# Channel attention and a relu² feed-forward: the later batches' folded weights by seven block products

## The chip, the cores and the metric

The kernel runs on one core of a Trainium2 chip. The metric is the device time of one execution in microseconds (us). A run's time here is that of the whole execution; the profiled execution also has a span, from its first to its last recorded instruction.

## The reference, cut to what matters

There are B = 4 batches of N = 6080 tokens with C = 256 channels, and F = 2048 hidden features, all float32.

```python
qn = q / (norm(q, axis=1) + 1e-6)          # norms over the tokens
kn = k / (norm(k, axis=1) + 1e-6)
s = kn.transpose(0, 2, 1) @ qn / tau       # 256 x 256 for each batch
a = softmax(s)                             # over the last axis
x = v @ a                                  # (4, 6080, 256)
h = maximum(x @ w_in, 0)                   # 256 -> 2048
out = (h * h) @ w_out                      # 2048 -> 256
```

## The kernel before

**Folding.** Since x only meets w_in, the kernel forms W = a w_in once a batch (256 x 2048) and computes v W. W is made in four groups g of 512 features. `eT` is the transposed softmax before its division by the row sums; the factor `rinv` (one over the row sum) is applied where W leaves PSUM.

**Precision.** TensorE takes float32 in a rounded form (fp32r). Every operand is therefore kept as a high part and a low part (`w_hi`, `w_lo`; `wi_hi`, `wi_lo`; `eT_hi`, `eT_lo`; `g_hi`, `g_lo`), and every product is three: high by high, high by low, low by high. The high part is a copy by ScalarE that rounds, the low part a difference by VectorE. For W the pair is the eviction of a PSUM tile: ScalarE writes `w_hi` (PSUM times `rinv`), VectorE then `w_lo` (PSUM times `rinv` less `w_hi`).

**The main loop.** A batch's tokens are cut into 12 blocks n (ten of 512 tokens, two of 480), and a block has 16 steps f, one for each 128 features, two steps a pair r. In a step `first_product` puts v W into a PSUM tile `ps_h` (6 matmuls of 512 columns) and ScalarE evicts it with relu into `x`. After a pair, `squares_and_sums` lets ScalarE square x, VectorE form sums of its blocks (`x<-x`), and both make `g_hi` and `g_lo`. The second product, two pairs later (LAG = 2), multiplies them with w_out by seven block products instead of eight (Strassen's scheme, `seven_products`; the sums of w_out are `wS`), into two PSUM tiles `ps_o`. At a block's end ScalarE copies `ps_o` out (`o<-ps_o`), and VectorE combines the pieces (`o<-o`).

**What runs beside it.** Batch b+1's attention and its W are generators, `attention(b)` and `softmax_and_W(b)`. The main loop takes one piece of them, up to the next `yield`, in each step but two of each block; in even steps right after `first_product`, in odd steps at the step's end. A group of the next batch's W may only be written once the last block of this batch is through with the old one (`may_write_W`), so its four groups are made during the last block, 11, and the start of the next batch's block 0. The softmax of batch 1 falls in blocks 8 and 9 of batch 0.

**PSUM.** There are eight banks: four for two `ps_o` tiles, three for `ps_h` (its three buffers also take the tiles of W and of the softmax), and one for the gram matrix, `ps_g`.

**Order.** Every engine carries out its instructions in the order in which the program issues them: `InProgramOrder` pins it, and so every row of the trace names its line, L27. The engines wait for each other by semaphores. The stretches of W in the old form are these lines of `softmax_and_W`:

```python
for h in range(NC):
    products(h)
    if h == NC - 1 and g + 1 < NG:
        wi[g + 1] = reload_w_in(b, g + 1)
    yield
    evict(h)
    yield
```

`products(h)` is six matmuls of 512 columns into one `ps_h` buffer (named `ps_w`), `reload_w_in` fetches the two parts of w_in's next group from a copy in DRAM.

Of the kernel before, what the change touches and what calls it, by code (L numbers as in the profile page):

```python
# [8 lines left out]
F32 = mybir.dt.float32  # L9
F32R = mybir.dt.float32r  # L10
# [20 lines left out]
def kernel(  # L31
# [25 lines left out]
    P = 128  # L57
# [92 lines left out]
    scratch = ctx.enter_context(tc.tile_pool(name="scratch", bufs=1, space=bass.MemoryType.DRAM))  # L150
    wi_kept = [[scratch.tile([P, NC, GRP], F32, name=f"wi_kept{g}_{i}") for i in range(2)] for g in range(NG)]

    def wi_tiles(b, g):
        hi = pool.tile([P, NC, GRP], F32R, tag="wi_hi", name=f"wi_hi{b}_{g}", bufs=1)
        lo = pool.tile([P, NC, GRP], F32R, tag="wi_lo", name=f"wi_lo{b}_{g}", bufs=1)
        return hi, lo
# [73 lines left out]
    def reload_w_in(b, g):  # L230
        parts = wi_tiles(b, g)
        for kept, part in zip(wi_kept[g], parts):
            nc.sync.dma_start(part.bitcast(F32), kept)
        return parts

# [139 lines left out]
    def attention(b):  # L375

        if b not in grams:
            grams[b] = Gram(b)
        g = grams[b]
        c0 = HEAD if b == 1 else 0  # L380
        for c in range(c0, min(c0 + QK_BUFS, g.n)):
            g.load(c)
        yield
        for c in range(c0, g.n):
            yield from until_even()
            p, jn, _ = g.q[c]
            hi = pool.tile([P, 2, J, C], F32R, tag="qk_hi", name=f"qk_hi{b}_{c}", bufs=1)
            lo = pool.tile([P, 2, J, C], F32R, tag="qk_lo", name=f"qk_lo{b}_{c}", bufs=1)
            h_, l_, r_ = (x[:p, :, :jn, :] for x in (hi, lo, g.raws[c]))
            scalar.copy(h_, r_)  # L390
            vector.tensor_sub(l_, r_, h_.bitcast(F32))
            yield
            yield from until_even()
            g.squares(c)
            g.add_squares(c)
            if c + QK_BUFS < g.n:
                g.load(c + QK_BUFS)
            for _ in g.products(c, [(hi, hi), (hi, lo), (lo, hi)]):
                yield
        yield from softmax_and_W(b)  # L400

    def pause(b, first, other):

        for _ in range(other if b else first):
            yield

    def softmax_and_W(b):
        gram, acc = grams[b].gram, grams[b].acc
        wi = {0: reload_w_in(b, 0)} if b else {}

        vector.tensor_add(acc[:, :, 0, :], acc[:, :, 0, :], acc[:, :, 1, :])
        yield from pause(b, 1, 2)
# [72 lines left out]
        vector.tensor_copy(eT_hi, ps_tv)  # L485
        vector.tensor_sub(eT_lo, ps_tv, eT_hi.bitcast(F32))
        yield from pause(b, 2, 3)

        for g in range(NG):
            while (b, g) not in may_write_W:  # L490
                yield
            if b == 0:
                while g not in wi_first:
                    yield
                hi, lo = wi_first.pop(g)
                keep_w_in(g, (hi, lo))
            else:
                hi, lo = wi.pop(g)
            w_hi = wpool.tile([P, NC, GRP], F32R, tag="w_hi", name=f"w_hi{b}_{g}")
            w_lo = wpool.tile([P, NC, GRP], F32R, tag="w_lo", name=f"w_lo{b}_{g}")  # L500
            ps_w = {}

            def products(h, terms=range(3)):
                if h not in ps_w:
                    ps_w[h] = ps_h.tile([P, T], F32, tag="h", name=f"ps_w{b}_{g}_{h}")
                for i in terms:
                    et, wt = ((eT_hi, hi), (eT_lo, hi), (eT_hi, lo))[i]
                    for d in range(NC):
                        tensor.matmul(
                            ps_w[h][:, 0:GRP],  # L510
                            et[:, d, h * P : (h + 1) * P],
                            wt[:, d, :],
                            start=i == 0 and d == 0,
                            stop=i == 2 and d == NC - 1,
                        )

            def evict(h):
                ps = ps_w.pop(h)[:, 0:GRP]
                scalar.activation(w_hi[:, h, :], ps, AF.Copy, scale=rinv[:, h : h + 1])
                vector.scalar_tensor_tensor(  # L520
                    w_lo[:, h, :],
                    ps,
                    rinv[:, h : h + 1],
                    w_hi[:, h, :].bitcast(F32),
                    op0=ALU.mult,
                    op1=ALU.subtract,
                )

            if b == 0:
                for h, terms in ((0, (0, 1)), (1, (0,)), (0, (2,)), (1, (1, 2))):  # L530
                    products(h, terms)
                yield
                for h in range(NC):
                    evict(h)
            else:
                for h in range(NC):
                    products(h)
                    if h == NC - 1 and g + 1 < NG:
                        wi[g + 1] = reload_w_in(b, g + 1)
                    yield  # L540
                    evict(h)
                    yield
            W[b, g] = w_hi, w_lo
            yield

# [367 lines left out]
```

## Time and profile before

| | before |
|---|---|
| median of 3 runs | 2214.52 us (2214.35 to 2214.86) |
| the profiled execution, its own time | 2215.23 us |
| its span | 2213.5 us |
| TensorE busy (PE) | 2205.0 us, 100% |
| VectorE busy (DVE) | 1774.4 us, 80% |
| ScalarE busy (ACT) | 1847.7 us, 83% |
| GpSimd busy (POOL) | 0.7 us |
| DMA, mean over the span | 57 GB/s |

PE is TensorE's matmuls, and PEld its weight loads, which run beside them; SP is the engine that issues DMAs. Matmuls are pipelined and overlap in the records, so their spacing (the difference of two starts) is what one of them occupies of TensorE. Rows of the trace name tiles without their numbers, as out<-in.

### The profile page before, as it was taken

The page shows a single profiled execution, that of the slowest core. Times are in us where ns is not written, and L with a number is a line of the kernel's source. Part 1 is how long each engine was busy: PE and PEld are TensorE (multiplying, and loading weights), DVE is VectorE, ACT ScalarE, POOL GpSimd, SP SyncE. Part 2 cuts the span into 40 slices and gives each one's busy share as a digit, 9 for nine tenths or more (in the row PEclk, how much of TensorE's full clock was granted, in tenths as well). Part 3 has the DMA queues.
Part 4 walks back from the last instruction along what each step waited for, and adds up shares of the span by engine and source line. Part 5 has one row for each costly group of instructions (what it writes and reads, how often), then busy time and mean ns, then how long its engine had stood idle before and what let it go on. Part 6 is the DMA issues. An engine that isn't in the chain of part 4 may idle for free.

```text
span 2213.5 us, 34513 instructions
## 1 busy us (share of the span) xinstructions
PE 2205.0 (100%) x13795; PEld 1982.1 (90%) x13795; DVE 1774.4 (80%) x2496; ACT 1847.7 (83%) x2300; POOL 0.7 (0%) x6
## 2 busy tenths in 40 slices
PE   9999999999999999999999999999999999999999
PEld 8788999989989999988998999998899888888898
DVE  6878888888778888878767888887877777787786
ACT  5788888888788888888878888888887888888887
POOL 0000000000000000000000000000000000000000
PEclk9999999999999999999999999999999999999999
DMA  9521122101121122110121222110102010010000
GB/s 340 181 77 38 60 74 68 46 19 38 57 67 58 61 69 65 61 41 22 36 76 48 63 68 72 58 53 22 35 23 76 21 37 20 22 36 20 21 27 18
DMA packets 76496, 127.01 MB, mean 57 GB/s; under 512 B 7728, under 2 KB 35120, under 8 KB 76336
## 3 DMA queue, kind: packets, MB, share of 16 engines
q1 hardware_dynamic: 76336, 124.81, 17.4%
q8 instruction: 108, 1.77, 0.3%
q14 instruction: 52, 0.43, 0.1%
HBM read 95.68 MB, written 29.10 MB: 56 GB/s over the span
## 4 chain that ended last, share of the span: by engine, by line
PE 96%; DMA 2%; DVE 1%; ACT 1%; SPq 0%; issue 0%; DVEq 0%; ACTq 0%
PE ps_h L27 47%; PE ps_o L27 42%; PE gram L27 4%; PE ps_w L27 2%; DMA qk<-in_k 1%; DMA qk<-in_q 0%; DVE dec_m L27 0%; DMA qk_heads<-in_q 0%; DMA w_raw<-in_w_in 0%; ACT x L27 0%; ACT g_hi L27 0%; SPq L268 0%; SPq L267 0%; DVE g_lo L27 0%; DVE wi_lo L27 0%
## 5 line engine op out<-in xcount | busy, mean ns | idle before, releaser
L27 DVE TENSOR_TENSOR g_lo<-x,g_hi 128x768 fp32r<-128x768 f32 (+2 forms) x749 | 808.8, 1080 | 78.9 <-ACT g_hi L27 78.2
L27 DVE TENSOR_TENSOR x<-x 128x512 f32<-128x512 f32 (+1 forms) x1095 | 558.4, 510 | 279.5 <-ACT x L27 253.8
L27 ACT CAST g_hi<-x 128x768 fp32r<-128x768 f32 (+2 forms) x749 | 701.8, 937 | 25.3 <-DVE x L27 12.3
L27 ACT ACTIVATE x<-ps_h 128x512 f32<-128x512 f32 (+1 forms) x768 | 455.8, 593 | 282.2 <-PE ps_h L27 264.1
L27 PE MATMUL ps_h<-v_hi,w_hi 128*128 128x512 f32 (+1 forms) x1536 | 478.4, 393 | 0.0
L27 PE MATMUL ps_h<-v_hi,w_lo 128*128 128x512 f32 (+1 forms) x1536 | 477.9, 392 | 0.0
L27 PE MATMUL ps_h<-v_lo,w_hi 128*128 128x512 f32 (+1 forms) x1536 | 475.0, 390 | 0.7 <-DVE v_lo L27 0.7
L27 ACT ACTIVATE x<-x 128x1024 f32<-128x1024 f32 (+1 forms) x384 | 404.5, 1053 | 11.9
L27 PE MATMUL ps_o<-g_lo,wS_hi 128*128 128x256 f32 (+1 forms) x1460 | 407.4, 279 | 0.0
L27 PE MATMUL ps_o<-g_hi,wS_lo 128*128 128x256 f32 (+1 forms) x1460 | 406.6, 279 | 0.0
L27 PE MATMUL ps_o<-g_hi,wS_hi 128*128 128x256 f32 (+1 forms) x1460 | 405.9, 278 | 0.0
L27 PEld LDWEIGHTS ps_h<-v_lo,w_hi 128*128 128x128 f32 x1536 | 287.8, 187 | 65.9 <-DVE v_lo L27 1.2
L27 PEld LDWEIGHTS ps_h<-v_hi,w_lo 128*128 128x128 f32 x1536 | 288.5, 188 | 62.4 <-DVE w_lo L27 0.3
L27 PE MATMUL ps_o<-g_hi,wo_hi 128*128 128x256 f32 (+2 forms) x1159 | 325.2, 285 | 0.0
L27 PE MATMUL ps_o<-g_hi,wo_lo 128*128 128x256 f32 (+2 forms) x1159 | 325.1, 285 | 0.0
L27 PE MATMUL ps_o<-g_lo,wo_hi 128*128 128x256 f32 (+2 forms) x1159 | 324.9, 285 | 0.0
L27 PEld LDWEIGHTS ps_o<-g_lo,wS_hi 128*128 128x128 f32 x1460 | 274.8, 188 | 16.1 <-DVE g_lo L27 0.2
L27 PEld LDWEIGHTS ps_o<-g_hi,wS_hi 128*128 128x128 f32 x1460 | 274.1, 188 | 15.6
L27 PEld LDWEIGHTS ps_o<-g_hi,wS_lo 128*128 128x128 f32 x1460 | 274.4, 188 | 0.0
L27 PEld LDWEIGHTS ps_h<-v_hi,w_hi 128*128 128x128 f32 x1536 | 238.2, 188 | 4.7
L27 PEld LDWEIGHTS ps_o<-g_hi,wo_hi 128*128 128x128 f32 x1159 | 218.4, 188 | 15.6
L27 PEld LDWEIGHTS ps_o<-g_lo,wo_hi 128*128 128x128 f32 x1159 | 217.7, 188 | 15.7 <-DVE g_lo L27 0.3
(96 smaller groups left out, 1689.2 us busy)
## 6 DMA issues: line engine op xcount, KB each, us to landing
qk<-in_k SPq DMA_DIRECT2D x87, 256.0 KB, 2.7
qk<-in_q SPq DMA_DIRECT2D x87, 256.0 KB, 3.0
v<-in_vT SPq DMA_DIRECT2D x40, 512.0 KB, 3.7
out_T<-o SPq DMA_DIRECT2D x152, 128.0 KB, 1.7
wi_hi<-wi_kept SPq DMA_DIRECT2D x12, 512.0 KB, 3.3
wi_lo<-wi_kept SPq DMA_DIRECT2D x12, 512.0 KB, 4.1
w_raw<-in_w_in SPq DMA_DIRECT2D x4, 1024.0 KB, 6.1
w_raw<-in_w_out SPq DMA_DIRECT2D x4, 1024.0 KB, 5.3
```

The lines of the kernel that those rows point to most:

```text
L27: return lambda *args, **kwargs: self.tc.keep_in_program_order(issue(*args, **kwargs))
```

## The change

Of batches 1 to 3, a group of W is no longer two tiles of six matmuls of 512 columns. eT and the group of w_in are each cut in 2 x 2 blocks, and seven block products of three matmuls with 256 columns each replace the eight that the old form holds. A group comes in two parts. The first holds four products (12 matmuls): two in the gram bank (`one`), two in a `ps_h` bank (`two`). ScalarE copies one quarter out, and VectorE forms three sums, each of the one before (`x[:, 1]` to `x[:, 3]`), and adds the first of them to both halves of `two` in PSUM. After two more pieces of the main loop the second part adds three products (9 matmuls) on top of `one` and `two`. One piece later the four quarters are evicted, by a `w_hi` and a `w_lo` of 256 columns each.

The products need sums of blocks on both sides. Those of eT (`e32`, `S`, `eS`) are made once a batch, after the softmax. Those of w_in are made once, beside batch 1's softmax (`sums_of_w_in`, put between its pieces by `beside_another`, in two of each five), and kept in DRAM (`wS_kept`); `reload_sums` fetches each group's, two groups ahead. To make them, w_in's two parts are read once more.

```diff
--- before.py
+++ after.py
@@ -150,6 +150,8 @@
     scratch = ctx.enter_context(tc.tile_pool(name="scratch", bufs=1, space=bass.MemoryType.DRAM))
     wi_kept = [[scratch.tile([P, NC, GRP], F32, name=f"wi_kept{g}_{i}") for i in range(2)] for g in range(NG)]
+    wS_kept = [[scratch.tile([P, 4, GRP // 2], F32, name=f"wi_sums_kept{g}_{i}") for i in range(2)] for g in range(NG)]
     def wi_tiles(b, g):
         hi = pool.tile([P, NC, GRP], F32R, tag="wi_hi", name=f"wi_hi{b}_{g}", bufs=1)
         lo = pool.tile([P, NC, GRP], F32R, tag="wi_lo", name=f"wi_lo{b}_{g}", bufs=1)
@@ -230,6 +232,52 @@
     def reload_w_in(b, g):
         parts = wi_tiles(b, g)
         for kept, part in zip(wi_kept[g], parts):
+            nc.sync.dma_start(part.bitcast(F32), kept)
+        return parts
+    def sums_of_w_in(b, wi):
+        half = GRP // 2
+        wi[0] = reload_w_in(b, 0)
+        yield
+        for g in range(NG):
+            hi, lo = wi.pop(g)
+            w = pool.tile([P, NC, GRP], F32, tag="qk", name=f"wi_raw{g}", bufs=QK_BUFS)
+            vector.tensor_add(w, hi.bitcast(F32), lo.bitcast(F32))
+            wi[(g + 1) % NG] = reload_w_in(b, (g + 1) % NG)
+            yield
+            S = pool.tile([P, 4, half], F32, tag="qk", name=f"wi_sums{g}", bufs=QK_BUFS)
+            vector.tensor_sub(S[:, 0:3:2, :], w[:, :, half:], w[:, 0, :].rearrange("p (k t) -> p k t", k=2))
+            vector.tensor_sub(S[:, 1, :], w[:, 1, half:], S[:, 0, :])
+            vector.tensor_sub(S[:, 3, :], w[:, 1, 0:half], S[:, 1, :])
+            yield
+            parts = wi_sums_tiles(b, 0, f"made{g}")
+            scalar.copy(parts[0], S)
+            yield
+            vector.tensor_sub(parts[1], S, parts[0].bitcast(F32))
+            for kept, part in zip(wS_kept[g], parts):
+                nc.sync.dma_start(kept, part.bitcast(F32))
+            yield
+        sums_made.append(b)
+    sums_made = []
+    def beside_another(main, side):
+        for k, _ in enumerate(main):
+            if k % 5 in (0, 2):
+                next(side, None)
+            yield
+    def wi_sums_tiles(b, i, name):
+        at = (dict(tag="qk_hi", bufs=1), dict(tag="qk_lo", bufs=1)) if i == 0 else (dict(tag="qk", bufs=QK_BUFS),) * 2
+        return [pool.tile([P, 4, GRP // 2], F32R, name=f"wiS{p}_{b}_{name}", **a) for p, a in enumerate(at)]
+    def reload_sums(b, g):
+        parts = wi_sums_tiles(b, g % 2, f"{g}")
+        for kept, part in zip(wS_kept[g], parts):
             nc.sync.dma_start(part.bitcast(F32), kept)
         return parts
@@ -397,16 +445,19 @@
                 g.load(c + QK_BUFS)
             for _ in g.products(c, [(hi, hi), (hi, lo), (lo, hi)]):
                 yield
-        yield from softmax_and_W(b)
+        if b == 1:
+            wi = {}
+            yield from beside_another(softmax_and_W(b, wi), sums_of_w_in(b, wi))
+        else:
+            yield from softmax_and_W(b, {0: reload_w_in(b, 0)})
     def pause(b, first, other):
         for _ in range(other if b else first):
             yield
-    def softmax_and_W(b):
+    def softmax_and_W(b, wi=None):
         gram, acc = grams[b].gram, grams[b].acc
-        wi = {0: reload_w_in(b, 0)} if b else {}
         vector.tensor_add(acc[:, :, 0, :], acc[:, :, 0, :], acc[:, :, 1, :])
         yield from pause(b, 1, 2)
@@ -485,6 +536,26 @@
         vector.tensor_copy(eT_hi, ps_tv)
         vector.tensor_sub(eT_lo, ps_tv, eT_hi.bitcast(F32))
         yield from pause(b, 2, 3)
+        if b:
+            room = pool.tile([P, 2, NC * C], F32, tag="acc", name=f"e_sums{b}", bufs=1)
+            e32, S = room[:, 0].rearrange("p (d c) -> p d c", d=NC), room[:, 1].rearrange("p (s c) -> p s c", s=4)
+            vector.tensor_add(e32, eT_hi.bitcast(F32), eT_lo.bitcast(F32))
+            yield
+            (A11, A12), (A21, A22) = [[e32[:, j, i * P : (i + 1) * P] for j in range(2)] for i in range(2)]
+            vector.tensor_add(S[:, 0], A21, A22)
+            vector.tensor_sub(S[:, 2], A11, A21)
+            vector.tensor_sub(S[:, 1], S[:, 0], A11)
+            vector.tensor_sub(S[:, 3], A12, S[:, 1])
+            yield
+            eS = pool.tile([P, 2, 4, P], F32R, tag="dec", name=f"eS{b}", bufs=1)
+            scalar.copy(eS[:, 0], S)
+            yield
+            vector.tensor_sub(eS[:, 1], S, eS[:, 0].bitcast(F32))
+            yield
+            while not sums_made:
+                yield
+            wS = {g: reload_sums(b, g) for g in range(2)}
         for g in range(NG):
             while (b, g) not in may_write_W:
@@ -533,13 +604,52 @@
                 for h in range(NC):
                     evict(h)
             else:
-                for h in range(NC):
-                    products(h)
-                    if h == NC - 1 and g + 1 < NG:
-                        wi[g + 1] = reload_w_in(b, g + 1)
-                    yield
-                    evict(h)
-                    yield
+                half = GRP // 2
+                Ts = wS.pop(g)
+                A = {f"A{i + 1}{j + 1}": [e[:, j, i * P : (i + 1) * P] for e in (eT_hi, eT_lo)] for i in range(2) for j in range(2)}
+                A.update({f"S{i + 1}": [eS[:, p, i] for p in range(2)] for i in range(4)})
+                D = {f"B{j + 1}{k + 1}": [w[:, j, k * half : (k + 1) * half] for w in (hi, lo)] for j in range(2) for k in range(2)}
+                D.update({f"T{i + 1}": [p[:, i, :] for p in Ts] for i in range(4)})
+                def product(ps, a, d, start=False, stop=False):
+                    for i, (x, y) in enumerate(((0, 0), (0, 1), (1, 0))):
+                        tensor.matmul(ps, A[a][x], D[d][y], start=start and i == 0, stop=stop and i == 2, skip_group_check=True)
+                one = ps_g.tile([P, NC, C], F32, tag="gram", name=f"ps_w{b}_{g}_0")
+                two = ps_h.tile([P, T], F32, tag="h", name=f"ps_w{b}_{g}_1").rearrange("p (k t) -> p k t", k=2)
+                x = pool.tile([P, 4, half], F32, tag="acc", name=f"w_sums{b}_{g}", bufs=1)
+                product(one[:, 0], "A11", "B11", start=True)
+                product(one[:, 1], "S2", "T2", stop=True)
+                product(two[:, 0], "S1", "T1", start=True)
+                product(two[:, 1], "S3", "T3")
+                scalar.copy(x[:, 0], one[:, 0])
+                vector.tensor_add(x[:, 1], one[:, 1], x[:, 0])
+                vector.tensor_add(x[:, 2], two[:, 0], x[:, 1])
+                vector.tensor_add(x[:, 3], two[:, 1], x[:, 2])
+                vector.tensor_add(two, two, x[:, 1:2, :].broadcast_to([P, 2, half]))
+                yield
+                yield
+                product(one[:, 0], "A12", "B21", stop=True)
+                product(two[:, 0], "S4", "B22")
+                product(two[:, 1], "A22", "T4", stop=True)
+                if g + 1 < NG:
+                    wi[g + 1] = reload_w_in(b, g + 1)
+                if g + 2 < NG:
+                    wS[g + 2] = reload_sums(b, g + 2)
+                yield
+                for h, k, src in ((0, 0, one[:, 0]), (0, 1, two[:, 0]), (1, 0, two[:, 1]), (1, 1, x[:, 3])):
+                    at = slice(k * half, (k + 1) * half)
+                    scalar.activation(w_hi[:, h, at], src, AF.Copy, scale=rinv[:, h : h + 1])
+                    vector.scalar_tensor_tensor(
+                        w_lo[:, h, at],
+                        src,
+                        rinv[:, h : h + 1],
+                        w_hi[:, h, at].bitcast(F32),
+                        op0=ALU.mult,
+                        op1=ALU.subtract,
+                    )
+                yield
             W[b, g] = w_hi, w_lo
             yield
```

Three places show how the instructions move. In the names, `g_lo_11_3` is block 11, pair 3; a `ps_w` or `w_sums` has its group as its first number; the last number of each only counts tiles.

On ScalarE, in block 11 of batch 1, where group 0 of batch 2's W is evicted. Before:

```order
L27 CAST g_hi_11_3_11010<-x_11_3_10976 128x720 [waits PE_49,Activation_49]
L27 ACTIVATE w_hi_0_10916<-ps_w_0_1_10978,rinv_10138 128x512
L27 ACTIVATE x_11_4_11041<-ps_h_11_8_11034 128x480 [waits DVE_49,PE_49]
L27 CAST g_hi_11_3_11010<-x_11_3_10976 128x960 [waits DVE_49]
L27 ACTIVATE x_11_4_11041<-ps_h_11_9_11058 128x480 [waits PE_49]
```

and after:

```order
L27 CAST g_hi_11_3_11217<-x_11_3_11177 128x720 [waits PE_49,Activation_49]
L27 ACTIVATE w_hi_0_11106<-ps_w_0_0_11108,rinv_10311 128x256
L27 ACTIVATE w_hi_0_11106<-ps_w_0_1_11109,rinv_10311 128x256
L27 ACTIVATE w_hi_0_11106<-ps_w_0_1_11109,rinv_10311 128x256 [waits DVE_49]
L27 ACTIVATE w_hi_0_11106<-w_sums_0_11110,rinv_10311 128x256
L27 ACTIVATE x_11_4_11254<-ps_h_11_8_11247 128x480 [waits PE_49]
L27 CAST g_hi_11_3_11217<-x_11_3_11177 128x960
L27 ACTIVATE x_11_4_11254<-ps_h_11_9_11271 128x480 [waits PE_49]
```

All four evictions of the group now stand between the two casts of g_hi, and the third waits for VectorE.

On VectorE, the same place and what follows it, up to where the second tile of group 0 and then the first of group 1 stood. Before:

```order
L27 TENSOR_TENSOR g_lo_11_3_11011<-x_11_3_10976,g_hi_11_3_11010 128x720
L27 TENSOR_TENSOR o_10_10876<-o_10_10876 128x240 x2
L27 SCALAR_TENSOR_TENSOR w_lo_0_10917<-ps_w_0_1_10978,rinv_10138,w_hi_0_10916 128x512
L27 TENSOR_TENSOR g_lo_11_3_11011<-x_11_3_10976,g_hi_11_3_11010 128x960
L27 TENSOR_TENSOR v_lo_0_11054<-v_0_10628,v_hi_0_11000 128x1024
L27 TENSOR_TENSOR x_11_4_11041<-x_11_4_11041 128x480
L27 TENSOR_TENSOR x_11_4_11041<-x_11_4_11041 128x240 x2
L27 TENSOR_TENSOR g_lo_11_4_11067<-x_11_4_11041,g_hi_11_4_11066 128x720
L27 TENSOR_TENSOR o_10_10876<-o_10_10876 128x240
L27 TENSOR_TENSOR o_10_10876<-o_10_10876 128x2x240
L27 SCALAR_TENSOR_TENSOR w_lo_1_11093<-ps_w_1_0_11094,rinv_10138,w_hi_1_11092 128x512
```

and after, from the differences on:

```order
L27 SCALAR_TENSOR_TENSOR w_lo_0_11107<-ps_w_0_0_11108,rinv_10311,w_hi_0_11106 128x256
L27 SCALAR_TENSOR_TENSOR w_lo_0_11107<-ps_w_0_1_11109,rinv_10311,w_hi_0_11106 128x256 x2
L27 SCALAR_TENSOR_TENSOR w_lo_0_11107<-w_sums_0_11110,rinv_10311,w_hi_0_11106 128x256
L27 TENSOR_TENSOR g_lo_11_3_11218<-x_11_3_11177,g_hi_11_3_11217 128x960
L27 TENSOR_TENSOR v_lo_0_11267<-v_0_10818,v_hi_0_11207 128x1024
L27 TENSOR_TENSOR x_11_4_11254<-x_11_4_11254 128x480
L27 TENSOR_TENSOR x_11_4_11254<-x_11_4_11254 128x240 x2
L27 TENSOR_TENSOR g_lo_11_4_11280<-x_11_4_11254,g_hi_11_4_11279 128x720
L27 TENSOR_TENSOR o_10_11066<-o_10_11066 128x240
L27 TENSOR_TENSOR w_sums_1_11309<-ps_w_1_0_11307,w_sums_1_11309 128x256
L27 TENSOR_TENSOR w_sums_1_11309<-ps_w_1_1_11308,w_sums_1_11309 128x256 x2
L27 TENSOR_TENSOR ps_w_1_1_11308<-ps_w_1_1_11308,w_sums_1_11309 128x512
```

The four differences of group 0 stand where one of 512 columns stood, and group 1's three sums and the addition in PSUM stand where its first difference stood (one more `o` row lies ahead of them).

On VectorE, in block 8 of batch 0, where batch 1's norms become `nr`. Before:

```order
L27 SCALAR_TENSOR_TENSOR nu_4193<-ns_4192,ny_4189 128x4
L27 SCALAR_TENSOR_TENSOR ny_4189<-nu_4193,ny_4189 128x4
L27 TENSOR_TENSOR g_lo_8_2_4165<-x_8_2_4142,g_hi_8_2_4164 128x1024
L27 TENSOR_TENSOR x_8_3_4201<-x_8_3_4201 128x512
L27 TENSOR_TENSOR x_8_3_4201<-x_8_3_4201 128x256 x2
```

and after:

```order
L27 SCALAR_TENSOR_TENSOR nu_4207<-ns_4206,ny_4203 128x4
L27 SCALAR_TENSOR_TENSOR ny_4203<-nu_4207,ny_4203 128x4
L27 TENSOR_TENSOR wi_sums_4220<-wi_raw_4092 128x2x256
L27 TENSOR_TENSOR wi_sums_4220<-wi_raw_4092,wi_sums_4220 128x256 x2
L27 TENSOR_TENSOR g_lo_8_2_4179<-x_8_2_4156,g_hi_8_2_4178 128x1024
L27 TENSOR_TENSOR x_8_3_4215<-x_8_3_4215 128x512
L27 TENSOR_TENSOR x_8_3_4215<-x_8_3_4215 128x256 x2
```

The three sums of w_in's group 0 now stand inside the chain of small operations that ends in `nr`.

## Rows read from the trace of the kernel before

**Rows 1.** The page: busy time by engine; the chain that ended last, by engine.

```profile
PE 2205.0 (100%) x13795; PEld 1982.1 (90%) x13795; DVE 1774.4 (80%) x2496; ACT 1847.7 (83%) x2300; POOL 0.7 (0%) x6
...
PE 96%; DMA 2%; DVE 1%; ACT 1%; SPq 0%; issue 0%; DVEq 0%; ACTq 0%
```

**Rows 2.** Timeline of TensorE: start, duration (us), instruction, count.

```profile
1142.38 0.63 PE L27 MATMUL ps_w<-wi_hi,eT_hi 128*128 128x512 f32 x2
1142.85 0.62 PE L27 MATMUL ps_w<-wi_hi,eT_lo 128*128 128x512 f32 x2
...
1723.56 0.28 PE L27 MATMUL ps_o<-g_hi,wS_hi 128*128 128x256 f32 x1
...
1724.96 0.64 PE L27 MATMUL ps_w<-wi_hi,eT_hi 128*128 128x512 f32 x2
```

**Rows 3.** Timeline of ScalarE in block 8 of batch 0; in brackets the idle time before.

```profile
469.75 0.84 ACT L27 ACTIVATE s<-gram,nr 128x256 f32<-128x256 f32 x2 [3.98 <-DVE nr L27]
470.48 1.05 ACT L27 CAST g_hi<-x 128x1024 fp32r<-128x1024 f32 x1
```

**Rows 4.** Groups by shape, VectorE: count | busy us, mean ns | idle before.

```profile
L27 DVE TENSOR_TENSOR x<-x 128x256 f32<-128x256 f32 x608 | 258.4, 425 | 20.9
...
L27 DVE TENSOR_TENSOR x<-x 128x512 f32<-128x512 f32 x304 | 210.1, 691 | 193.7 <-ACT x L27 193.0
```

**Rows 5.** Timeline of ScalarE and VectorE, block 11 of batch 1.

```profile
1132.26 0.68 ACT L27 ACTIVATE w_hi<-ps_w,rinv 128x512 fp32r<-128x512 f32 x1
1132.84 0.56 ACT L27 ACTIVATE x<-ps_h 128x480 f32<-128x480 f32 x1
...
1134.60 0.74 DVE L27 SCALAR_TENSOR_TENSOR w_lo<-ps_w,rinv,w_hi 128x512 fp32r<-128x512 f32 x1
1135.26 1.15 DVE L27 TENSOR_TENSOR g_lo<-x,g_hi 128x960 fp32r<-128x960 f32 x1
1136.33 1.22 DVE L27 TENSOR_TENSOR v_lo<-v,v_hi 128x1024 fp32r<-128x1024 f32 x1
1137.46 1.54 DVE L27 TENSOR_TENSOR x<-x 128x480 f32<-128x480 f32 x3
...
1140.75 0.74 DVE L27 SCALAR_TENSOR_TENSOR w_lo<-ps_w,rinv,w_hi 128x512 fp32r<-128x512 f32 x1
```

**Rows 6.** DMA issues: count, size of one, median us to landing.

```profile
wi_lo<-wi_kept SPq DMA_DIRECT2D x12, 512.0 KB, 4.1
```

**Rows 7.** Timeline of VectorE, ScalarE and TensorE, block 0 of batch 2.

```profile
1162.15 1.61 DVE L27 TENSOR_TENSOR x<-x 128x512 f32<-128x512 f32 x3 [2.50 <-ACT x L27]
...
1164.55 0.74 DVE L27 SCALAR_TENSOR_TENSOR w_lo<-ps_w,rinv,w_hi 128x512 fp32r<-128x512 f32 x1
...
1163.47 0.59 ACT L27 ACTIVATE x<-ps_h 128x512 f32<-128x512 f32 x1
...
1168.02 0.96 ACT L27 COPY o<-ps_o 128x960 f32<-128x960 f32 x1
...
1170.56 0.28 PE L27 MATMUL ps_o<-g_hi,wS_hi 128*128 128x256 f32 x1
```

**Rows 8.** Timeline of ScalarE and TensorE, block 8 of batch 0.

```profile
473.88 0.59 ACT L27 ACTIVATE x<-ps_h 128x512 f32<-128x512 f32 x1
...
474.52 0.76 PE L27 MATMUL ps_h<-v_hi,w_hi 128*128 128x512 f32 x2
```

**Rows 9.** Timeline of ScalarE and TensorE, block 9's start.

```profile
492.39 1.00 ACT L27 COPY o<-ps_o 128x1024 f32<-128x1024 f32 x1
...
494.22 0.28 PE L27 MATMUL ps_o<-g_hi,wS_hi 128*128 128x256 f32 x1
```

**Rows 10.** Timeline of VectorE and TensorE, block 9 of batch 0.

```profile
515.95 1.23 DVE L27 TENSOR_TENSOR g_lo<-x,g_hi 128x1024 fp32r<-128x1024 f32 x1 [0.25 <-ACT g_hi L27]
...
520.98 0.28 PE L27 MATMUL ps_o<-g_lo,wS_hi 128*128 128x256 f32 x1
```

**Rows 11.** Stretch: length, busy us (count) of PE, PEld, DVE, ACT, POOL; clock; DMA; GB/s.

```profile
1119.00:1145.00 26.00, 26.00 (x160) 23.46 (x159) 20.77 (x33) 19.23 (x26) 0.00 (x0) 1.00 0.27 84
```

## The prediction

> **What bounds the kernel now.** The page's totals come first [rows 1]: TensorE is busy for 2205.0 us, all of the span to the rounding, and the chain that ended last runs through TensorE for 96%. VectorE (80%) and ScalarE (83%) have air, but not everywhere. So two questions decide: how much TensorE time the seven products save, and whether the work that they add to VectorE and ScalarE makes TensorE wait in places where those two are nearly full. The second needs the timeline. Every stretch below is of the kernel before, and 0.2% (4.4 us) is about what a measurement of this kernel can tell from no change.
>
> **The saving on TensorE.** A group of W takes 12 matmuls of 512 columns before and 21 of 256 after. In the timeline two 512-column matmuls start 0.47 us after the two before them (1142.38, 1142.85), 0.2325 us each; twelve of 256 columns, each with a weight load of its own, fill 1723.56 to 1724.96, 0.1167 us each [rows 2]. That is 2.79 against 2.45 us: 0.34 us a group, and 12 groups (four for each of batches 1, 2 and 3) give 4.1 us. More than this the change can't save, as nothing else leaves TensorE.
>
> The Trainium skill's page "TensorE: Matmul & The Clock Gate", section "Back-to-back issue gap", puts an isolated matmul at N/2.4 + 2.5 ns, and warns that the weight load sets the spacing too. By that formula the saving would be an estimated 3.6 us; the rows measure both spacings, 9% and 8% wider than the formula's, and the sum goes by them.
>
> **What is added to each group.** ScalarE had two evictions of 512 columns; it gets one copy and four evictions of 256 columns. The scaling of the gram tile is an operation of that shape: two of them start at 469.75 and what follows at 470.48 [rows 3], so 0.37 us from start to start. VectorE had two differences of 512. It gets three dependent sums of 256 columns (0.425 us each [rows 4], 0.455 with the hand-over), an addition of 512 columns into PSUM (0.69, [rows 4]) and four differences of 256. That makes 2.05 us for the chain of sums. A difference of 512 columns takes 0.66 us from start to start (1134.60 to 1135.26 [rows 5]), and 256 columns less save 0.27 (0.69 against 0.42), so I take 0.385. Addition into PSUM is in no row: its lower end is 0.69, that of SBUF, its upper end twice that, and I take the lower, as w_lo, which reads PSUM in 512 columns, takes only 0.74 [rows 5]. The DMAs (of the sums 16 of 512 KB in batch 1, 8 stores and 8 loads, and 8 loads in each later batch; 8 more loads of w_in in batch 1) are issued on SP a group or more ahead. Loads of that size land in 4.1 us [rows 6], less than the time of two steps. I cost them at nothing, and 4 us once if SP is held up.
>
> **First stall: the second part of group 1.** TensorE may start it only after the chain of sums. I follow VectorE in batch 2 [rows 5]; W's matmuls lie at the same distances in batches 1 and 3. Up to the differences of group 0 all is 0.35 us earlier than before, so the first stands at 1134.25. The order shows the third eviction on ScalarE waiting for VectorE, and it can only be the second difference, since the two read one PSUM tile. So ScalarE, which reaches its second eviction at 1132.3 (1132.26 [rows 5], less 0.35 and plus 0.37), stands until VectorE has done two differences, at 1134.25 + 0.385 + 0.47 = 1135.1. Then come evictions three and four (0.37 each), the eviction of ps_h (0.56 [rows 5] less 0.1 that overlaps) and the cast of g_hi (1.0, by the 1.05 of 1024 columns in [rows 3]), until 1137.35. The g_lo that follows the differences in VectorE's order needs that cast and ends its turn at 1138.45. Before, v_lo started at 1136.33: VectorE is now 2.1 us later. It then does v_lo (1.13 from start to start), x, g_lo and o (together 3.29, 1137.46 to 1140.75) without a pause until 1142.9, and the sums until 1144.95. TensorE gets to the second part's first product at 1142.03 (before, h=1 started at 1142.38, and group 0 saved 0.35), and three matmuls later, at 1142.38, it needs the last sum. It waits 2.6 us, 7.7 for three batches. Without the third eviction's wait the same walk gives 1.0; with differences of 0.66 it gives 3.7.
>
> Before, too, an eviction and its difference of one tile lie apart: w_hi from 1132.26 for 0.68 us, w_lo from 1134.60 [rows 5]. The Trainium skill's page "PSUM — Partial Sum Buffer", section "PSUM bank collisions raise a hardware error", says that two engines must not touch one bank at once, reads against reads included. By the rule the wait stays in each eviction, and the first stall is 2.6 us; if the two engines could read side by side it would be 1.0.
>
> **Second stall: the copies of ps_o.** Group 2's evictions fall where a block of tokens ends. Before, ScalarE takes ps_h at 1163.47 and copies the second half of ps_o from 1168.02 to 1168.98; TensorE overwrites that half at 1170.56, so 1.6 us are to spare [rows 7]. After, the third eviction waits for VectorE's x and g_lo (1162.15 to 1164.55) and two differences (0.855), until 1165.4, and ps_h follows two evictions later, at 1166.14. The copy is 2.7 us late and TensorE waits 1.1 us; 3.3 for three batches. Its ends are 0 and 1.5 a batch.
>
> Groups 0 and 3 I cost at nothing: by the same walk their sums end 2.8 and 1 us before TensorE wants them.
>
> **Third stall: making w_in's sums beside batch 1's softmax.** It adds to VectorE, four times, 1.14 (w, 1024 columns, by v_lo), 1.6 (three sums) and 1.14 us (the low half), and to ScalarE a cast of 1.05 [rows 3]. The softmax's own sums add 1.75 us (one of 512 columns, four of 128: another 0.13 off the 0.42, so 0.29 each) and 0.6 once a batch. The place is the fullest one before the change.
> - ScalarE stands 3.98 us for nr [rows 3] and evicts ps_h only at 473.88; the next first product starts at 474.52, the moment its bank is free (473.88 + 0.59) [rows 8]. The sums of group 0 (1.6 us) come just before nr on a VectorE that has no pause there. TensorE waits 1.6 us.
> - Two more low halves and sums put VectorE's x at the start of block 9 about 4.3 us later, so that ScalarE's copy of ps_o is 3.6 us late, with 0.8 us to spare (492.39 + 1.0 against 494.22 [rows 9]) and TensorE itself 1.5 us later: 1.3 us.
> - In block 9 the pairs f = 6 to 11 get 1.14 + 1.14 + 1.75 + 1.6 = 5.6 us more. Before, the g_lo that ends at 517.18 is wanted at 520.98 [rows 10]: 3.8 us to spare. 1.8 us go beyond it; I take 2.5, as VectorE comes in late from the copies.
>
> Together 5.4 us, between 0 (if what there is to spare absorbs all of it) and 7. Batches 2 and 3 have only the softmax's own sums, and stay within what there is to spare.
>
> **The sum.** -4.1 + 7.7 + 3.3 + 5.4 = +12.3 us. The profiled execution took 2215.23 us (span 2213.5 and 1.7 around it), so it would take 2227.5; it lay 0.7 above the median of the runs, 2214.52, and the forecast for a median is 2226.8.
>
> **The rivals.**
> - *Only the first stall is real* (the sums and copies are absorbed by double buffers): -4.1 + 7.7 = +3.6, 2218.1 us. For it: g_lo has 3.8 us to spare even in the full stretch. Against: TensorE starts at 474.52 with nothing to spare.
> - *Everything hides*, the other side: 2210.4 us. The one mechanism is that VectorE finishes group 1's sums before 1142.38, 2.6 us earlier than my walk. It decides from there: at 2.6 us less each batch gains, and with the other two stalls gone as well the 4.1 us remain. For it: VectorE is busy for 20.77 of 26 us from 1119 to 1145 [rows 11]. Against: its pauses there are spent before the differences, not after them.
> - *The stalls feed each other*: ScalarE and VectorE wait for each other in each eviction, and a late ps_h eviction delays the first product too, since the second PSUM tile leaves ps_h two buffers instead of three. At 3.7 us for the first stall, 1.5 for the second and 7 for the third: -4.1 + 11.1 + 4.5 + 7 = +18.5, 2233 us.
>
> **How the numbers follow.** The forecast has 66% (its own range 2219 to 2231), the dearer case 13%, the first stall alone 15% (3% of it over 2219), all hidden 6% (1% faster by over 0.2%, for which even the whole saving falls short). So slower 0.82, the same 0.17, faster 0.01. The range leaves out some 10% on each side: 2216 to 2234, from two thirds of the first stall's effect to the dearer end.
>
> **What would show it.** Right: the row of ps_w in 256 columns at the spacing of ps_o; waits of TensorE for VectorE's sums at group 1 of each batch, near 2.6 us; waits for ScalarE's copy of ps_o, near 1 us, a block boundary later; several waits between 470 and 530 us; ScalarE waiting for w_lo in each eviction. Wrong: a TensorE as busy as before and a span under 2211, or waits at groups 0 and 3, or waits for a DMA of the sums.

## The result, and the profile after

The changed kernel takes 2230.51 us (median of six runs, 2229.27 to 2231.89), the kernel before 2214.34 us (median of six, 2214.02 to 2214.86): 0.7% slower, ratio 1.0072 (1.0062 to 1.0083). The forecast was 2226.8 us and its range 2216 to 2234. The profiled execution took 2231.89 us, its span is 2230.1 us.

The page of the changed kernel: span, busy time by engine, and the chain that ended last by engine.

```profile
span 2230.1 us, 34975 instructions
...
PE 2209.4 (99%) x13903; PEld 1987.0 (89%) x13903; DVE 1819.7 (82%) x2606; ACT 1861.2 (83%) x2343; POOL 0.7 (0%) x6
...
PE 89%; DVE 6%; ACT 3%; DMA 1%; issue 1%; SPq 0%; DVEq 0%; ACTq 0%
```

Against [rows 1] the chain now runs for 9% through VectorE and ScalarE, which before had 2%: TensorE waits for them. What it waited for most, in the changed kernel (us in total, times, longest):

```profile
PE ps_w L27 <- DVE w_sums L27: 3.4, 3, 1.1
PE ps_w L27 <- DVE ps_w L27: 3.3, 3, 1.1
PE ps_o L27 <- ACT o L27: 3.2, 8, 0.7
PE ps_o L27 <- DVE g_lo L27: 3.1, 4, 1.2
```

The list has five more entries, none over 1.1 us, and no load of the stored sums is among them. Where the time went is read from the starts of the blocks: the start of a block's first product, in the trace of the changed kernel less that in the trace of before. The changed execution happened to begin its blocks 0.89 us earlier.

| stretch | later by | what lies in it |
|---|---|---|
| batch 0, blocks 0 to 7 | 0.0 us | nothing of the change |
| batch 0, blocks 8 and 9 | 6.0 us | softmax of batch 1, w_in's sums |
| W of batch 1 | 4.5 us | 573 to 640 us |
| W of batch 2 | 4.4 us | 1119 to 1187 us |
| W of batch 3 | 3.0 us | 1666 to 1736 us |

Together 17.9 us. First the saving. The two parts of a group at which nothing waits (timeline of TensorE, group 0 in block 11 of batch 1: the first product of each part, and the first one of the main loop behind it):

```profile
1129.31 0.28 PE L27 MATMUL ps_w<-wi_hi,eT_hi 128*128 128x256 f32 x1
1130.75 0.28 PE L27 MATMUL ps_o<-g_hi,wo_hi 128*128 128x240 f32 x1
...
1135.71 0.28 PE L27 MATMUL ps_w<-wi_hi,eT_hi 128*128 128x256 f32 x1
1136.78 0.27 PE L27 MATMUL ps_o<-g_hi,wo_hi 128*128 128x240 f32 x1
```

That is 1.44 and 1.07 us. TensorE at group 1's second part, in batch 1 (timeline: start, duration, count, in brackets the wait before):

```profile
600.82 0.27 PE L27 MATMUL ps_o<-g_hi,wo_lo 128*128 128x240 f32 x1
602.23 0.38 PE L27 MATMUL ps_w<-wi_hi,eT_hi 128*128 128x256 f32 x1 [1.13 <-DVE w_sums L27]
602.46 0.28 PE L27 MATMUL ps_w<-wi_lo,eT_hi 128*128 128x256 f32 x1
602.57 0.28 PE L27 MATMUL ps_w<-wi_hi,eT_lo 128*128 128x256 f32 x1
603.96 0.39 PE L27 MATMUL ps_w<-wi_hi,eS 128*128 128x256 f32 x1 [1.10 <-DVE ps_w L27]
```

The first product comes 1.30 us later than the spacing of its neighbours asks for, the second 1.27: 2.6 us, twice more in the other batches. VectorE at that place, its three sums and the addition into PSUM:

```profile
601.76 1.41 DVE L27 TENSOR_TENSOR w_sums<-ps_w,w_sums 128x256 f32<-128x256 f32 x3
603.20 0.70 DVE L27 TENSOR_TENSOR ps_w<-ps_w,w_sums 128x512 f32<-128x512 f32 x1
```

The wait has two halves: the second part's first product, which writes into `one`, starts when VectorE is through with the first sum, which reads `one`; the fourth matmul starts when the addition into `two` has ended. ScalarE and VectorE ahead of it, where group 0 is evicted (timeline of the changed kernel, to be laid beside [rows 5], which are of batch 2, 546 us later):

```profile
590.77 0.83 ACT L27 ACTIVATE w_hi<-ps_w,rinv 128x256 fp32r<-128x256 f32 x2
594.02 0.48 ACT L27 ACTIVATE w_hi<-ps_w,rinv 128x256 fp32r<-128x256 f32 x1 [2.41 <-DVE w_lo L27]
...
595.24 0.99 ACT L27 CAST g_hi<-x 128x960 fp32r<-128x960 f32 x1
...
593.12 0.87 DVE L27 SCALAR_TENSOR_TENSOR w_lo<-ps_w,rinv,w_hi 128x256 fp32r<-128x256 f32 x2
...
596.27 1.16 DVE L27 TENSOR_TENSOR g_lo<-x,g_hi 128x960 fp32r<-128x960 f32 x1 [0.85 <-ACT g_hi L27]
597.34 1.22 DVE L27 TENSOR_TENSOR v_lo<-v,v_hi 128x1024 fp32r<-128x1024 f32 x1
```

Read it as a ring: ScalarE's third eviction waits 2.41 us for VectorE's second difference; the cast of g_hi stands behind it; VectorE's g_lo waits 0.85 us for that cast. In all, ScalarE waits 17.3 us for w_lo in twelve groups. One block boundary later the copy of ps_o ends late, and TensorE with it (changed kernel, batch 1, beside [rows 7]; the second half of ps_o):

```profile
633.12 0.95 ACT L27 COPY o<-ps_o 128x960 f32<-128x960 f32 x1
...
634.13 0.39 PE L27 MATMUL ps_o<-g_hi,wS_hi 128*128 128x256 f32 x1 [0.59 <-ACT o L27]
```

In block 8 of batch 0, where the chain of small operations ends in `nr`, TensorE waits in two steps (changed kernel, beside [rows 3]):

```profile
470.32 0.84 ACT L27 ACTIVATE s<-gram,nr 128x256 f32<-128x256 f32 x2 [4.68 <-DVE nr L27]
471.05 1.05 ACT L27 CAST g_hi<-x 128x1024 fp32r<-128x1024 f32 x1
...
472.15 0.39 PE L27 MATMUL ps_o<-g_hi,wS_hi 128*128 128x256 f32 x1 [0.23 <-ACT g_hi L27]
473.41 0.39 PE L27 MATMUL ps_o<-g_lo,wS_hi 128*128 128x256 f32 x1 [0.87 <-DVE g_lo L27]
```

Last, stretches of the changed kernel right after group 1's waits (length; PE, PEld, DVE, ACT, POOL busy; granted clock as a share of 2.4 GHz; DMA share; GB/s):

```profile
604.00:605.00 1.00, 1.00 (x7) 0.96 (x8) 1.00 (x2) 0.00 (x0) 0.00 (x0) 0.99 0.00 0
605.00:607.00 2.00, 2.00 (x6) 1.65 (x5) 1.93 (x4) 0.00 (x0) 0.00 (x0) 0.50 0.76 223
607.00:608.00 1.00, 1.00 (x6) 0.99 (x5) 0.23 (x1) 0.76 (x2) 0.00 (x0) 0.50 1.03 414
608.00:609.00 1.00, 1.00 (x8) 0.96 (x7) 0.78 (x2) 0.55 (x2) 0.00 (x0) 0.81 1.00 381
```

After the two waits the granted clock is 0.50, the level of 1.2 GHz, until about 608.4 us. The same stands in batch 2 and not in batch 3, and W of batches 1 and 2 costs 1.6 and 1.4 us more than W of batch 3. Of the six runs, two with a mean granted clock of 1.000 took 2229.3 us, two with 0.999 2230.3 and 2230.7, and two with 0.998 2231.9.

### The profile page after: what moved, and what is told of

Same layout as the page of the kernel before. It is cut to its first block, busy times and chain, and to the rows that moved or that the text cites. A ratio compares the mean times of both kernels' runs of the same rounds, so it can differ in the third digit from the quotient of the medians.

```text
span 2230.1 us, 34975 instructions
## 1 busy us (share of the span) xinstructions
PE 2209.4 (99%) x13903; PEld 1987.0 (89%) x13903; DVE 1819.7 (82%) x2606; ACT 1861.2 (83%) x2343; POOL 0.7 (0%) x6
## 4 chain that ended last, share of the span: by engine, by line
PE 89%; DVE 6%; ACT 3%; DMA 1%; issue 1%; SPq 0%; DVEq 0%; ACTq 0%
PE ps_h L27 44%; PE ps_o L27 39%; PE gram L27 4%; PE ps_w L27 1%; DVE x L27 1%; DVE g_lo L27 1%; ACT x L27 1%; DVE acc L27 1%; DMA qk<-in_k 1%; ACT g_hi L27 1%; DVE o L27 0%; DMA qk<-in_q 0%; DVE dec_m L27 0%; DVE v_lo L27 0%; ACT o L27 0%
```

## The experiments

**Of the change only w_in's sums.** W keeps two tiles of six matmuls; the softmax's own sums are left out, and the stored sums are read by nothing.

```diff
-        yield from softmax_and_W(b)
+        if b == 1:
+            wi = {}
+            yield from beside_another(softmax_and_W(b, wi), sums_of_w_in(b, wi))
```

> W in the old form (12 matmuls of 512 columns a group), and of the change only w_in's sums: made beside batch 1's softmax and stored, never read. My theory: the third stall is made by VectorE's added work alone. TensorE waits as in the changed kernel near 472, 493 and 515 to 525 us, 5.4 us in all, with its restarts 6.0: 2214.3 + 6.0 = 2220.3 us, and nothing waits at W. Rival: the sums hide, and what the changed kernel loses there comes of the seven products' tiles and loads: 2214.3 us.

Measured: 2218.88 us against 2214.31 (ratio 1.0020, 1.0011 to 1.0030). By block starts blocks 8 and 9 are 4.5 us longer and nothing else is. TensorE waits at the same places as in the changed kernel except the last one, the 1.4 us that end at 525.96 us there. So the third stall is made by the sums and not by the seven products: 4.5 us of it are w_in's sums, and 1.5 come only when the softmax's own sums are added to them, which the expectation had not separated. How much of the 4.5 us VectorE's operations make and how much ScalarE's cast for each group, this run doesn't part.

**The order of the evictions.**

```diff
-for h, k, src in ((0, 0, one[:, 0]), (0, 1, two[:, 0]), (1, 0, two[:, 1]), (1, 1, x[:, 3])):
-    scalar.activation(w_hi[:, h, at], src, ...)
-    vector.scalar_tensor_tensor(w_lo[:, h, at], src, ...)
+for q_ in quarters:
+    high(*q_)
+for q_ in quarters:
+    low(*q_)
```

> The changed kernel with one order altered: ScalarE is given all four w_hi of a group first, then VectorE all four w_lo, so that no w_hi stands behind a w_lo. The work is the same. My theory: ScalarE's waits for w_lo (17.3 us in twelve) vanish, group 1's wait falls from 2.6 to 1.0 us a batch, the waits for the copies of ps_o (1.1 a batch) go, and the slow TensorE clock after group 1's wait goes or stays: 2230.5 - 3 x 2.7 = 2222.4 us, or 2219.5 without the slow clock. Rival: VectorE's added work alone makes both waits; they stay, 2230 us.

Measured: 2220.67 us (ratio 1.0029, 1.0017 to 1.0040). ScalarE at the same place in batch 2 of this kernel, and what TensorE waits for at W in all of it:

```profile
1137.50 1.20 ACT L27 ACTIVATE w_hi<-ps_w,rinv 128x256 fp32r<-128x256 f32 x3
1138.58 0.51 ACT L27 ACTIVATE w_hi<-w_sums,rinv 128x256 fp32r<-128x256 f32 x1
1138.98 0.58 ACT L27 ACTIVATE x<-ps_h 128x480 f32<-128x480 f32 x1
...
PE ps_w L27 <- DVE ps_w L27: 2.7, 3, 0.9
```

The work is the same, ScalarE no longer waits, group 1's wait is 1.07 us a batch and the waits at W's block boundaries are gone, as is the slow clock in the profiled execution (of the six runs one, the slowest at 2222.76 us, has a mean clock of 0.999). By block starts W now costs nothing (0.0 us a batch). The ring of waits made all of the second stall and 1.5 of the first one's 2.6 us. For the 1.07 us that are left VectorE's added work is the explanation by the prediction's walk, which has 1.0 there without the ring; no run takes that work away.

**w_in's sums later.** They are made after the softmax, one piece in each step.

```diff
-            yield from beside_another(softmax_and_W(b, wi), sums_of_w_in(b, wi))
+            yield from softmax_and_W(b, wi)
...
-            while not sums_made:
-                yield
+            if b == 1:
+                yield from sums_of_w_in(b, wi)
```

> The changed kernel with w_in's sums made after batch 1's softmax, a piece in each step, instead of between its pieces. My theory: the waits between 470 and 530 us go (6.0 us with restarts), and in their new place, 525 to 575 us, VectorE and the chain have room, since there it is busy for 36.1 of 48 us before: 2224.5 us, up to 2227 if some of the 15.5 us of sums do not fit into the 11.9 free ones. Rival: work on VectorE costs the same wherever it is put: 2230.5 us.

Measured: 2245.12 us (ratio 1.0138, 1.0123 to 1.0153). The old waits are gone, and worse ones came. Between 550 and 580 us TensorE waits for g_lo (up to 1.8 us at once), with stretches at the low clock; and the sums, stored only then, were not back when W wanted them (timeline of TensorE):

```profile
583.80 0.41 PE L27 MATMUL ps_w<-wi_hi,eT_lo 128*128 128x256 f32 x1
588.65 0.58 PE L27 MATMUL ps_w<-wiS,eS 128*128 128x256 f32 x1 [4.44 <-DMA wiS<-wi_sums_kept]
591.72 1.65 PE L27 MATMUL ps_w<-wiS,eS 128*128 128x256 f32 x6 [2.49 <-DMA wiS<-wi_sums_kept]
```

My expectation failed: free time added up over a stretch is not room for a piece in each step. The trace shows two ways in which g_lo comes late. In one pair of steps VectorE has two pieces ahead of it (a low part and the next addition, from 556.18 to 558.45 us). In the next pair ScalarE's cast of the sums stands behind VectorE's sums, and g_hi's behind that cast, the same ring as in the evictions (both engines in this kernel):

```profile
563.43 1.05 ACT L27 CAST wiS_made<-wi_sums 128x1024 fp32r<-128x1024 f32 x1 [3.16 <-DVE wi_sums L27]
564.38 0.99 ACT L27 CAST g_hi<-x 128x960 fp32r<-128x960 f32 x1
...
562.51 0.88 DVE L27 TENSOR_TENSOR wi_sums<-wi_raw,wi_sums 128x256 f32<-128x256 f32 x2
565.40 1.16 DVE L27 TENSOR_TENSOR g_lo<-x,g_hi 128x960 fp32r<-128x960 f32 x1 [2.01 <-ACT g_hi L27]
```

The last experiment comes back to it.

**One more piece of the main loop in group 1**, and then two more.

```diff
                 yield
+                if g == 1:
+                    yield
                 yield
                 product(one[:, 0], "A12", "B21", stop=True)
```

> The changed kernel with one more piece of the main loop between the two parts of group 1 of each batch. My theory: VectorE's sums end 2.6 us after TensorE wants them, and a step of the main loop is some 2.6 us of TensorE's work: the waits for w_sums and ps_w at group 1 (2.76 us a batch with their restarts) go, and so does the slow clock that follows them (1.4 to 1.6 us in two of the three batches): 2230.5 - 8.3 - 3.0 = 2219.2 us. The copies' waits stay or shift with group 2. Rival: VectorE is behind as a whole, and the wait only moves to the next product that needs it: 2230 us.

Measured: 2224.77 us (ratio 1.0046, 1.0029 to 1.0062). The wait for w_sums and the slow clock are gone, that for ps_w stayed (1.26 us a batch): the piece reached lies right after the next first product, and only 1.3 us of TensorE's work had come between. A new wait of 0.93 us for group 3's w_lo appeared.

> The changed kernel with two more pieces of the main loop between the parts of group 1 instead of the fourth experiment's one. There the wait for the last sum stayed (1.27 us a batch), since the one piece put only a first product between, and group 3's w_lo came 0.93 us too late for the first product that reads it. My theory: group 1's wait goes altogether (3 x 1.4 us with restarts), but group 3 comes another 2.6 us later: 2224.8 - 4.1 + 3 x 2.6 = 2228.5 us, and 2220.7 if group 3 keeps its place. Rival: VectorE is short of time as a whole, and the wait for the sums stays.

Measured: 2229.80 us (ratio 1.0069, 1.0055 to 1.0082). Group 1's second part waits no more, and group 3 is late: its second part waits for the sums at 643 us (0.94 and 1.26 us), and in two batches a first product waits for w_hi. Postponing a group moves the wait; the time is 1.3 us above the one expected, and the place, group 3's sums, was not foreseen.

**w_in's sums on GpSimd.**

```diff
-            vector.tensor_add(w, hi.bitcast(F32), lo.bitcast(F32))
+            pool_engine.tensor_add(w, hi.bitcast(F32), lo.bitcast(F32))
```

and so for the other sums and the two parts.

> The changed kernel with all of w_in's sums (their additions, differences, high and low parts) on GpSimd instead of VectorE and ScalarE, in the same places. My theory: the waits at 472, 493 and 515 to 519 us (4.5 us, as in the first experiment) go: 2230.5 - 4.5 = 2226.0 us; the wait of 1.4 us at 525 us goes too if the softmax's own sums fit alone: 2224.5. Rival: a busy GpSimd lengthens VectorE's operations, or is itself late, and the waits stay or grow: 2230 us or more, with VectorE's rows longer than theirs in the kernel before.

Measured: 2244.49 us (ratio 1.0133, 1.0119 to 1.0147); the rival holds. While GpSimd works, VectorE's operations grow; the timeline of both engines in this kernel:

```profile
462.63 3.26 POOL L27 TENSOR_TENSOR wiS_made<-wi_sums,wiS_made 128x1024 fp32r<-128x1024 f32 x1
465.86 2.81 POOL L27 TENSOR_TENSOR wi_raw<-wi_hi,wi_lo 128x1024 f32<-128x1024 f32 x1
468.74 1.32 POOL L27 TENSOR_TENSOR wi_sums<-wi_raw 128x512 f32<-128x512 f32 x1
...
463.56 6.79 DVE L27 TENSOR_TENSOR x<-x 128x512 f32<-128x512 f32 x3
```

VectorE's three sums take 6.79 us where they took 1.61 [rows 7]; TensorE then waits up to 4.6 us for g_lo. Not all of the loss is such waits: from 440 to 490 us the mean granted clock is 0.83, which by an estimate (17% of 50 us) makes up to 8.5 of the 19.4 us that blocks 8 and 9 lose. The Trainium skill's page "SBUF — State Buffer", section "Who interferes with whom", says that the two engines share a pair of ports, which one instruction holds to its end, and that a tensor_tensor with both inputs in SBUF contends with GpSimd's reads. The rows agree that VectorE's operations with both inputs in SBUF lengthen beside GpSimd's; of ports they show nothing.

**Order of evictions, one more piece, and GpSimd** together.

> The changed kernel with the second experiment's order of evictions, the fourth's one more piece in group 1 and w_in's sums on GpSimd. My theory: no wait is left but perhaps the softmax's sums at 525 us, and only the saving of 12 x 0.29 us remains: 2214.3 - 3.5 = 2210.8 us, or 2212.2 with that wait. Rival: each fix moves its wait to the next buffer (group 3's w_lo, the copies of ps_o), and it is no faster than the kernel before: 2214 to 2217 us.

Measured: 2230.39 us (ratio 1.0073, 1.0059 to 1.0087). With GpSimd blocks 8 and 9 lose 19.4 us, again partly by the clock (0.86 from 440 to 490 us). Of the forecast only W's part is right: each batch's W is 1.12 us shorter than before, with no wait.

**Each load of the stored sums issued twice.**

```diff
             nc.sync.dma_start(part.bitcast(F32), kept)
+            nc.sync.dma_start(part.bitcast(F32), kept)
```

> The changed kernel with each load of the stored sums issued twice, 24 more loads of 512 KB. My theory: the change's DMAs are hidden, and twice as many are too: 2230.5 us. Rival: the added traffic is part of the loss (some 20 MB more than before), and doubling the larger half of it shows: 2232 us or more, with waits of TensorE for a DMA.

Measured: 2232.75 us (ratio 1.0082, 1.0068 to 1.0096). The time is the rival's, but TensorE waits for a load only once, 2.2 us in batch 1 at 579 us; in batches 2 and 3 W costs what batch 3's did in the changed kernel, 2.9 us. The second line is what SP, which issues the loads, waits for (both of this kernel):

```profile
PE ps_w L27 <- DMA wiS<-wi_sums_kept: 2.2, 1, 2.2
SPq L282 <- DMA wiS<-wi_sums_kept: 48.6, 24, 6.2
```

Each second load of a tile waits until the first has landed, so a tile comes about twice as late, and the run doesn't show what the traffic alone would cost. The tile that TensorE waits for had landed from its first load when SP issued the second, at 573.97 us, and is wanted at 579.4: without the second load some 5 us are to spare (an estimate). So the changed kernel's loads are hidden.

**Order and one more piece, sums on VectorE.**

> The changed kernel with the second experiment's order of evictions and the fourth's one more piece in group 1, w_in's sums again on VectorE as in the changed kernel. My theory: W of each batch is now a gain of 1.12 us, as between the same blocks of the seventh experiment, and only batch 1's sums are left as a loss of 6.0 us: 2214.4 + 6.0 - 3.4 = 2217.0 us, with no wait at ps_w. Rival: what GpSimd hid in the seventh experiment (other times for the same steps) comes back as waits at W, and it stays at 2220.7 us, that of the second experiment.

Measured: 2217.65 us (ratio 1.0013, 1.0004 to 1.0022), within 0.7 us of my theory. No wait at ps_w; by block starts batch 1's sums cost 6.0 us and W gives back 1.12 us a batch.

**The sums spread out, seven products for batches 2 and 3.** Beside the two fixes:

```diff
+    def slowly(gen):
+        for _ in gen:
+            yield
+            yield
...
+        if b in (1, 2):
+            yield from slowly(sums_of_w_in(b, wi, (0, 1) if b == 1 else (2, 3)))
```

> As the ninth, but seven products for batches 2 and 3 only (batch 1 keeps twelve matmuls of 512 columns a group), and w_in's sums made in smaller pieces, one in two steps, after the softmax: groups 0 and 1 at the end of batch 0, groups 2 and 3 at the end of batch 1. My theory: a pair of steps has room for one piece of at most 1.2 us there, nothing waits, and 2 x 1.12 us are saved: 2214.4 - 2.2 = 2212.2 us. Rival: the sums cost some time wherever VectorE and ScalarE feed TensorE, as the third experiment's did, or their loads come late: 2215 us or more.

Measured: 2212.25 us (median of 11) against 2214.56 (median of 21), ratio 0.9990 (0.9981 to 0.9999): faster than both kernels, by little. All that TensorE waits for in it lies in the first 80 us; by block starts nothing is lost anywhere, and each of the two W gives 1.12 us. The stretch in which the third experiment lost, in that one and then in this (columns as above):

```profile
525.00:575.00 50.00, 45.73 (x284) 40.84 (x283) 42.46 (x63) 34.69 (x45) 0.00 (x0) 0.97 0.46 162
```

```profile
525.00:575.00 50.00, 50.00 (x332) 46.36 (x331) 42.40 (x64) 44.10 (x57) 0.00 (x0) 1.00 0.31 106
```

VectorE is equally busy, 42.4 of 50 us, but not with the same work: some 13 us of it are w_in's sums in the third experiment's stretch and some 5 in this one, since this kernel makes two groups at the end of batch 0 and the other all four. The other also got through less of the main loop in the same 50 us (284 matmuls against 332). In the third experiment g_lo stands behind two pieces, or ScalarE behind VectorE's sums; here one piece at most stands ahead of g_lo, the cast comes when its sums have ended, and TensorE goes without a pause. Spacing, size of a piece and number of groups changed together, and no run here parts them.

## Why the prediction was right, and where it was off

The direction, the range and the three places were right; the paths of some waits were others than forecast, and two terms were missing from the sum.

- **The saving**: forecast 0.34 us a group, measured 0.28. The two parts of an undisturbed group fill 1129.31 to 1130.75 and 1135.71 to 1136.78, 2.51 us for 21 matmuls, 0.1195 each where I took 0.1167. That is 3.4 us in all, not 4.1. (The two spacings that I took are 8% and 7% wider than the quoted formula gives, not 9% and 8%; the sum doesn't use it.)
- **The first stall**: forecast 2.6 us a batch, the profile has 1.30 and 1.27. I had only the wait for the last sum; that the first product already waits for the first sum, whose PSUM bank it writes, was not in the walk. The total is set by the end of the sums either way. The walk's mechanism (ScalarE held by the second difference, the late cast, the late g_lo) stands in the rows above, and the second experiment undid it. Forecast 1.0 without that wait, measured 1.07. The rule of the Trainium skill's page "PSUM — Partial Sum Buffer", section "PSUM bank collisions raise a hardware error", that two engines must not read one bank at once, was kept in every kernel here, so no run shows what would happen without it. The row that I gave for it, w_lo at 1134.60 in the kernel before, is no sign of it: there VectorE is busy with operations ahead of w_lo until that time.
- **The second stall**: forecast 1.1 a batch at the second half of ps_o, measured 0.36 at the first half and 0.76 at the second. That the total agrees is in part luck.
- **The third stall**: forecast 5.4 us, measured 6.0 by block starts. The waits themselves are 1.5, 1.2 and 2.7 us at the three places named. At the first, the cause is the one forecast (ScalarE, kept longer by nr), the path is not: no first product waits for its bank. TensorE stops earlier, in the second product, 0.40 us for the g_hi whose cast stands behind the scaling by nr and 1.14 us for the g_lo that follows. So the 1.6 us there were right for a path that I had wrong.
- **Addition into PSUM**: I took the lower end, 0.69 us; it is 0.70, in all twelve.
- **The DMAs** at nothing: right, no wait in the changed kernel, though the loads of the sums land in 5.6 us and not 4.1.
- **What was missing**: by block starts the loss is 17.9 us where the sum said 12.3 (the profiled execution's early start took 0.9 of it back). Of these 5.6 us the slow clock made 3.0 (1.6 and 1.4), which the sum put at nothing, and the smaller saving 0.7. The rest is TensorE's restarts: a first matmul after a wait lasts 0.38 or 0.39 us where the next lasts 0.28, so 0.1 us goes with each of 19 waits (seven in blocks 8 and 9, four in each W), 1.9 us. So the price of a wait was mis-sized: I took it as the wait alone. The median, 16.2 us above that of before, has less of the slow clock than the profiled execution.

Two expectations of the experiments were wrong on the same matter: that one more piece alone would end group 1's waits (the fourth experiment; together with the order of evictions it did), and that free VectorE time can be filled at will (the third).

## What to carry to other kernels

When two engines evict the same PSUM tile in turn, give the first engine all its reads before the second's: here the order alone was worth 10 us of 16, up to 3 of them the slow clock's. Free time added up over a stretch says little about side work beside a packed engine: look at what stands ahead of each hand-over, on both engines that feed it, and don't give one of them an operation on what the other has only just been given. A saving of 0.28 us a group is less than any of the waits of 0.36 to 1.36 us here, so first find the place where nothing waits, and only then count matmuls.

## What the runs showed of the hardware

Two waits of 1.3 us with three matmuls between them came with 3.4 us of TensorE at 1.2 GHz (clock 0.50) in two of three batches of the changed kernel's profiled execution. The same two waits stand in each batch of the profiled executions of three experiments: of those places two of three had such a stretch in the third, one of three in the one with GpSimd alone, and none in the one with each load issued twice. A single wait of 1.07 or 1.26 us in each batch (the second and fourth experiments) was followed by none in their profiled executions. What decides these runs don't tell. GpSimd's additions of 1024 columns took 3.1 us on average (VectorE's 1.22), and beside GpSimd's work VectorE's sums took up to four times their time (6.79 against 1.61 us). A first matmul of 256 columns after a wait was followed by the next 0.23 us later instead of 0.12. VectorE's addition of 512 columns into PSUM costs what one in SBUF does, 0.70 against 0.69 us.
